# Bias relus with the first weight as a second scalar, in an attention and experts kernel

## The chip, the cores and the metric

The kernel runs on one core of a Trainium2 chip. The metric is device time in microseconds (us) of one execution; several executions were timed and one was profiled. PE is TensorE's matmuls, PEld its weight loads, DVE VectorE, ACT ScalarE, POOL GpSimd, and SP the engine whose queue issues the DMAs (SPq).

## The reference

Three blocks run one after the other, all in float32.

```python
scores = scale * np.matmul(q, k.transpose(0, 1, 3, 2))      # batch 2, 8 heads, 576 positions, head size 64
psi_rel = np.log1p(np.abs(rel))                             # rel = i - j
psi_i = np.log1p(np.maximum(pos[:, None], 1.0))
x = (psi_rel / psi_i)[..., None]
h = np.maximum(x @ w1 + b1, 0.0)                            # 32 hidden values
bias = h @ w2                                               # one bias per head, row i and column j
attn = softmax(scores + bias);  out = attn @ v
# then, on 1152 tokens of 512 values:
x = sum over 4 experts of p[e] * (relu(x @ w1[e]) @ w2[e])  # 1024 hidden values each
result = ((x @ w_a) * (x @ w_b)) @ w_out                    # 1536 hidden values
```

The change lies in the bias. Since the bias of row i depends on |i − j| alone, one row needs a table of log1p(0 ... 575). The kernel takes the division by psi_i out of the relu: max(t·w1/psi_i + b1, 0) is max(t·w1, −b1·psi_i)/psi_i + b1. So a row's relu is a maximum of the scaled table with one number per hidden value; the second matmul follows, then the factor 1/psi_i and a correction w2·b1 that is the same for all rows.

## The kernel before

**Bias units.** A unit is 16 rows i, of 36 units. Its hidden values lie on the 128 partitions as 4 rows i of 32 values each, so a unit takes four relus (`bias_group`, lines 367 to 378), each on `n` columns of the table; n falls from 576 (unit 0) to 304 in the middle and rises again to 576. In units 0 to 7 every even one has its fourth relu on ScalarE, with the other three on VectorE; the odd ones have all four on VectorE; later units have three and one. The buffers of the relus (`hh`) are eight. TensorE multiplies by `w2s` into PSUM (`pb`, line 390), an engine copies one side out with the row factor `rinv` and the correction `corr` (`put`, lines 408 and 410), another mirrors the other side (`mirror`, line 239), and a DMA on SP's queue stores the unit to memory (line 421). Attention loads tiles of it back (`bt`, lines 476 to 487) and adds them in the reduction of line 516.

**Constants.** One DMA brings `cs`: the table `tab`, the values psi_i (`neg_`), the row factors `rinv`, the two columns `cw` (w1 and b1) and `w2s`. ScalarE scales the whole table by w1 (line 345). VectorE makes the ScalarE biases `pos` (line 340), the VectorE bounds `neg_`, in place (line 341), and multiplies `w2s` by 8 (line 342), since the scores are kept eight times as large. TensorE then multiplies `w2s` by b1 (line 353), and VectorE copies that into `corr`, one vector for units with one relu on ScalarE and one for units with none, in which the quarter of ScalarE's row is set to 0 (lines 357 to 359). The relus of both engines wait for both the scaled table and the bounds.

**Order.** A planner (`Plan.run`, line 147) simulates the five engines with written costs and due times (`op`, with `prio`) and emits each engine's instructions in the order it finds; on the chip every engine works through its own list in that order and waits on semaphores. Bias units 0 to 7 have the highest rank, then 8 to 15, then the rest, which are mixed with attention steps (line 513 on) and with the experts (`up` line 772, the activation's low half `hl` line 796, weight splits `wl` line 658, `pz` line 785). From about 70 us on TensorE's list is filled with expert matmuls.

Of the kernel before, what the change touches and what calls it, by code (L numbers as in the profile page):

```python
# [9 lines left out]
F32 = mybir.dt.float32  # L10
U32 = mybir.dt.uint32
F32R = mybir.dt.float32r
AF = mybir.ActivationFunctionType
ALU = mybir.AluOpType
# [3 lines left out]
B, H, S, D = 2, 8, 576, 64  # L18
HID = 32
P = 128  # L20
# [21 lines left out]
ENGINES = {"kcast": "ACT DVE", "ksub": "POOL DVE", "qcast": "DVE", "qsub": "DVE", "pt": "ACT DVE", "tail": "ACT DVE", "side": "ACT DVE", "mirror": "POOL ACT", "mirror0": "ACT DVE",  # L42
           "whi": "ACT DVE", "wlo": "DVE", "xhi": "DVE", "xlo": "POOL DVE", "rb": "ACT DVE", "rx": "ACT DVE", "s64": "DVE",
           "wsum": "POOL DVE", "whi2": "ACT", "wlo2": "DVE", "px": "ACT DVE", "xsum": "DVE", "xhi2": "ACT", "xlo2": "DVE", "hmul": "DVE", "hlo": "DVE"}
# [49 lines left out]
class Plan:  # L94
# [9 lines left out]
    def op(self, eng, fn, r=(), w=(), rw=(), hold=(), prio=0, lock=False, after=(), size=0, late=0):  # L104

        o = Op()
        o.eng, o.fn, o.prio, o.lock, o.size = eng, fn, prio, lock, size
        o.after, o.n, o.done, o.late = [], len(self.ops), False, late
        deps = set(after)
        for b in r:  # L110
            deps.update(b.writers)
        for b in rw:
            deps.update(b.writers)
            deps.update(b.readers)
        for b in rw:
            b.writers, b.readers = [o], []
        for b in w:
            b.writers.append(o)
        for b in r:
            b.readers.append(o)  # L120
        deps.discard(o)
        o.left = len(deps)
        for d in deps:
            d.after.append(o)
        o.bufs = list({id(b): b for b in (*r, *w, *rw, *hold)}.values())
        for b in o.bufs:
            b.left += 1
        self.ops.append(o)
        return o
# [102 lines left out]
def tile_kernel(ctx, tc, qd, kd, kf, vd, cst, probs, w1r, w2r, war, wbr, wor, out):  # L232
    nc = tc.nc
    plan = Plan()
    op = plan.op
    engine = {"ACT": nc.scalar, "DVE": nc.vector, "POOL": nc.gpsimd}

    def copy(e, out, in_):
        (nc.scalar.copy if e == "ACT" else engine[e].tensor_copy)(out, in_)  # L239
# [10 lines left out]
    def t_psum(n, engs="ACT DVE"):  # L250
        est = {"ACT": n / 1.2 + 55, "DVE": n / 0.96 + 68}
        return {e: est[e] for e in engs.split()}

    def tp(stack, name, **kw):
        return stack.enter_context(tc.tile_pool(name=name, bufs=1, reuse_waits="tile", **kw))
# [29 lines left out]
    hp = tp(hp_stack, "hp", side="right")  # L285
# [45 lines left out]
    NG = S // 4  # L331
    cs_t = hp.tile([P, S + NG + NU + 2 + 32], F32, name="cs")
    cs, pos = Buf(t=cs_t), hp.tile([P, NU, max(RELUS.values())], F32, name="pos")
    corr = {n: hp.tile([P, 1], F32, name=f"corr{n}") for n in range(max(RELUS.values()) + 1)}
    tab, neg_ = cs_t[:, 0:S], cs_t[:, S:S + NG]
    rinv, cw, w2s = cs_t[:, S + NG:S + NG + NU], cs_t[:, S + NG + NU:S + NG + NU + 2], cs_t[:, S + NG + NU + 2:]
    op({"SP": 440}, lambda e: nc.sync.dma_start(out=cs_t, in_=cst), w=[cs], size=P * 3160)

    def scales(e):
        nc.vector.tensor_scalar(out=pos, in0=neg_.rearrange("p (u g) -> p u g", g=4)[:, :, 4 - pos.shape[2]:], scalar1=cw[:, 1:2], scalar2=None, op0=ALU.mult)  # L340
        nc.vector.tensor_scalar(out=neg_, in0=neg_, scalar1=cw[:, 1:2], scalar2=-1.0, op0=ALU.mult, op1=ALU.mult)
        nc.vector.tensor_scalar(out=w2s, in0=w2s, scalar1=8.0, scalar2=None, op0=ALU.mult)

    lg = Buf(t=cs_t)
    op({"ACT": S / 1.2 + 200}, lambda e: nc.scalar.activation(out=tab, in_=tab, func=AF.Copy, scale=cw[:, 0:1]), r=[cs], w=[lg], prio=-1)
    op({"DVE": 450}, scales, r=[cs], w=[lg])
    cs = lg
    pc, cr = new("tv", "pc"), Buf(t=cs_t)


    def corr_mm(e):
        for g in range(4):
            nc.tensor.matmul(pc.t[32 * g:32 * g + 32, 0:1], w2s, cw[:, 1:2], start=True, stop=True)

    def corr_copy(e):
        for n, x in corr.items():
            nc.vector.tensor_copy(x, pc.t[:, 0:1])
            for g in range(4 - n, 4):
                nc.vector.memset(x[32 * g:32 * g + 32], 0.0)

    def dist(u):
        before, after = 16 * u + 15, S - 16 * u
        return before, after, max(before + 1, after)
# [3 lines left out]
    def bias_group(u, rank):  # L367
        pri, acts = RANK[rank], RELUS[rank] if u % 2 == 0 or rank != "bias0" else 0
        before, after, n = dist(u)
        hs = []  # L370
        for g in range(4):
            G = 4 * u + g
            hh = new("hh")
            hs.append(hh)
            if g < 4 - acts:
                op({"DVE": n / 1.92 + 130}, lambda e, hh=hh, G=G: nc.vector.tensor_scalar(out=hh.t[:, :n], in0=tab[:, :n], scalar1=neg_[:, G:G + 1], scalar2=None, op0=ALU.max), r=[cs], w=[hh], prio=pri, lock=True)  # L376
            else:
                op({"ACT": n / 1.2 + 220}, lambda e, hh=hh, G=G: nc.scalar.activation(out=hh.t[:, :n], in_=tab[:, :n], func=AF.Relu, bias=pos[:, u, g - 4:][:, :1]), r=[cs], w=[hh], prio=pri)
        pb = new("tv" if n <= 512 else "s", "pb")
        bst = new("bst")  # L380


        def base():
            return (pb.t, 0) if n <= 512 else (pb.t.rearrange("p a b -> p (a b)"), 512 - n // 2)

        def mm(e):
            t, o = base()
            for lo, hi in ((0, n),) if n <= 512 else ((0, n // 2), (n // 2, n)):
                for g in range(4):
                    nc.tensor.matmul(t[32 * g:32 * g + 32, o + lo:o + hi], w2s, hs[g].t[:, lo:hi], start=True, stop=True)  # L390

        op({"PE": n * 1.67 + 170}, mm, r=[*hs, cs], w=[pb], hold=[bst], prio=pri)


        def ends():
            t, o = base()
            b = bst.t
            if before >= after:
                side = b[:, 0:before + 1], t[:, o:o + 1 + before][:, ::-1]
                rest = b[:, before + 1:before + after], b[:, before - after + 1:before][:, ::-1]  # L400
            else:
                side = b[:, before:before + after], t[:, o:o + after]
                rest = b[:, 0:before], b[:, before + 1:2 * before + 1][:, ::-1]
            return side, rest

        def put(e, out, src):
            if e == "ACT":
                nc.scalar.activation(out=out, in_=src, func=AF.Identity, scale=rinv[:, u:u + 1], bias=corr[acts])  # L408
            else:
                nc.vector.tensor_scalar(out=out, in0=src, scalar1=rinv[:, u:u + 1], scalar2=corr[acts], op0=ALU.mult, op1=ALU.add)  # L410

        def mirror(e):
            copy(e, *ends()[1])

        m = min(before, after - 1)
        side = op({e: v + 95 for e, v in t_psum(n, ENGINES["side"]).items()}, lambda e: put(e, *ends()[0]), r=[pb, cr], w=[bst], prio=pri)
        op({e: v for e, v in {"POOL": 2 * m + 150, "ACT": m / 1.2 + 95, "DVE": m / 0.96 + 68}.items() if e in ENGINES["mirror0" if rank == "bias0" else "mirror"].split()}, mirror, w=[bst], after=[side], prio=pri)
        rows.append(Buf(t=bias_d))

        def store(e):  # L420
            nc.sync.dma_start(out=bias_d[16 * u:16 * u + 16, :, S - before:S + after].rearrange("i h j -> (i h) j"), in_=bst.t[:, :before + after])

        o = op({"SP": 440}, store, r=[bst], w=[rows[u]], prio=pri, size=P * 4 * (before + after))
        if u == P // 16 - 1:
            early.append(o)
# [707 lines left out]
    for b in range(B):  # L1133
        QK[0, b, 0] = plain(0, b)
    op({"PE": 600}, corr_mm, r=[cs], w=[pc])
    op({"DVE": 400}, corr_copy, r=[pc], w=[cr])
    for u in range(NU):
        bias_group(u, "bias0" if u < P // 16 else "bias1" if u < 256 // 16 else "bias2")
    for g in groups:
# [225 lines left out]
```

## Time and profile before

| | us |
|---|---|
| median of 3 timed executions | 791.68 (790.96 to 793.36) |
| the profiled execution, its own time | 791.38 |
| its span, first to last instruction | 789.6 |
| PE busy | 774.2 (98%) |
| PEld busy | 662.3 (84%) |
| DVE busy | 649.5 (82%) |
| ACT busy | 404.3 (51%) |
| POOL busy | 28.1 (4%) |

A matmul is pipelined and the end of one is modelled, so a busy PE isn't PE at its peak. The busy share is a mean over stages: in the first 70 us bias and attention follow each other over all engines; behind 300 us PE multiplies expert and output weights almost alone. Lines such as L376 are those of the kernel before.

### The profile page before, as it was taken

The page shows a single profiled execution, that of the slowest core. Times are in us where ns is not written, and L with a number is a line of the kernel's source. Part 1 is how long each engine was busy: PE and PEld are TensorE (multiplying, and loading weights), DVE is VectorE, ACT ScalarE, POOL GpSimd, SP SyncE. Part 2 cuts the span into 40 slices and gives each one's busy share as a digit, 9 for nine tenths or more (in the row PEclk, how much of TensorE's full clock was granted, in tenths as well). Part 3 has the DMA queues.
Part 4 walks back from the last instruction along what each step waited for, and adds up shares of the span by engine and source line. Part 5 has one row for each costly group of instructions (what it writes and reads, how often), then busy time and mean ns, then how long its engine had stood idle before and what let it go on. Part 6 is the DMA issues. An engine that isn't in the chain of part 4 may idle for free.

```text
span 789.6 us, 13146 instructions
## 1 busy us (share of the span) xinstructions
PE 774.2 (98%) x4933; PEld 662.3 (84%) x4933; DVE 649.5 (82%) x1374; ACT 404.3 (51%) x848; POOL 28.1 (4%) x46
## 2 busy tenths in 40 slices
PE   7998999999999999999999999999999999999997
PEld 3475678888988888888888888889889999999996
DVE  7899986889896687998989998988698985757545
ACT  6877765677766543544544535344466532433321
POOL 0000100000000000000000000010010100000000
PEclk9999999999999999999999999999999999999999
DMA  6996658677563134455545653545405340301103
GB/s 233 327 344 215 232 178 276 218 243 244 179 208 98 45 96 127 134 166 175 160 126 159 204 175 120 166 132 161 134 1 183 112 160 1 107 27 55 54 1 120
DMA packets 46432, 120.31 MB, mean 152 GB/s; under 512 B 5024, under 2 KB 9376, under 8 KB 46368
## 3 DMA queue, kind: packets, MB, share of 16 engines
q1 hardware_dynamic: 46224, 119.34, 46.6%
q8 instruction: 39, 0.64, 0.3%
q14 instruction: 25, 0.20, 0.1%
q10 hardware_dynamic: 144, 0.13, 0.0%
HBM read 93.62 MB, written 25.84 MB: 151 GB/s over the span
## 4 chain that ended last, share of the span: by engine, by line
PE 90%; DVE 6%; ACT 1%; issue 1%; DMA 1%; DVEq 0%; ACTq 0%
PE pz L785 32%; PE up L883 14%; PE pw L1030 9%; PE up L772 8%; PE pb L390 4%; PE pv L613 4%; PE pr L1030 4%; PE ps L513 4%; PE pt L548 4%; PE pq L1030 2%; PE ps L531 1%; PE pz L1110 1%; DVE pr L516 1%; DVE k L453 1%; PE rp L593 1%
## 5 line engine op out<-in xcount | busy, mean ns | idle before, releaser
L785 PE MATMUL pz<-wh,hh 128*128 128x512 f32 x386 | 153.2, 397 | 0.0
L785 PE MATMUL pz<-wh,hl 128*128 128x512 f32 x386 | 151.3, 392 | 0.0
L785 PE MATMUL pz<-wl,hh 128*128 128x512 f32 x386 | 151.2, 392 | 0.0
L785 PEld LDWEIGHTS pz<-wl,hh 128*128 128x128 f32 x386 | 72.5, 188 | 15.9
L785 PEld LDWEIGHTS pz<-wh,hh 128*128 128x128 f32 x386 | 72.5, 188 | 14.2 <-issue 1.8
L785 PEld LDWEIGHTS pz<-wh,hl 128*128 128x128 f32 x386 | 72.5, 188 | 12.2
L239 ACT COPY ct<-pw 128x640 f32<-128x640 f32 (+3 forms) x48 | 27.9, 582 | 85.0 <-PE pw L1030 85.0
L516 DVE CUSTOM_DVE_ANT_0 pr<-ps,bt 128x576 f32<-128x576 f32 (+1 forms) x80 | 59.9, 753 | 13.9 <-PE ps L513 11.3
L658 DVE TENSOR_TENSOR wl<-wst,wh 128x1024 fp32r<-128x1024 f32 (+1 forms) x60 | 69.7, 1162 | 1.9 <-ACT wh L239 1.6
L526 ACT ACTIVATE pr<-pr,sums 128x576 f32<-128x576 f32 x72 | 56.1, 780 | 15.3 <-DVE sums L516 10.4
L772 PE MATMUL up<-x_h,wh 128*128 128x256 f32 (+1 forms) x200 | 61.7, 308 | 0.7 <-DVE hl L796 0.7
L239 ACT CAST wh<-wst 128x1024 fp32r<-128x1024 f32 (+1 forms) x56 | 54.5, 974 | 15.1 <-PE pz L785 7.8
L772 PE MATMUL up<-x_h,wl 128*128 128x256 f32 (+1 forms) x200 | 57.3, 286 | 0.0
L772 PE MATMUL up<-x_l,wh 128*128 128x256 f32 (+1 forms) x200 | 57.2, 286 | 0.0
L239 ACT COPY ptb<-pt 128x512 f32<-128x512 f32 (+3 forms) x98 | 40.3, 438 | 30.8 <-PE pt L548 25.4
L376 DVE TENSOR_SCALAR hh<-cs 128x560 f32<-128x560 f32 (+17 forms) x112 | 43.9, 448 | 3.8 <-PE pb L390 3.6
L239 ACT COPY ct<-up 128x448 f32<-128x448 f32 x39 | 20.7, 531 | 47.8 <-PE up L883 47.6
L613 PE MATMUL pv<-ptb,v 128*64 128x128 f32 (+2 forms) x480 | 44.1, 331 | 0.3 <-ACT bst L408 0.3
L883 PE MATMUL up<-xb,wsh 128*128 128x448 f32 x156 | 44.3, 365 | 0.0
L1125 DVE TENSOR_TENSOR acc<-pz,acc 128x512 f32<-128x512 f32 x44 | 30.2, 689 | 15.9 <-PE pz L785 14.9
L772 PEld LDWEIGHTS up<-x_h,wh 128*128 128x128 f32 x200 | 37.6, 188 | 6.5 <-issue 3.0
L548 PE MATMUL pt<-ident,pr 128*128 128x128 f32 x288 | 41.7, 275 | 0.0
(194 smaller groups left out, 1844.8 us busy)
## 6 DMA issues: line engine op xcount, KB each, us to landing
wst<-in_w1r SPq DMA_DIRECT2D x30, 512.0 KB, 4.4
wst<-in_w2r SPq DMA_DIRECT2D x30, 512.0 KB, 4.5
bias_d<-bst SPq DMA_DIRECT2D x36, 295.5 KB, 4.1
bt<-bias_d SPq DMA_DIRECT2D x15, 576.0 KB, 5.3
v<-in_vd SPq DMA_DIRECT2D x24, 320.0 KB, 4.3
s<-in_war SPq DMA_DIRECT2D x12, 512.0 KB, 4.9
wz_d<-hl SPq DMA_DIRECT2D x24, 256.0 KB, 2.5
s<-in_wbr SPq DMA_DIRECT2D x12, 512.0 KB, 4.9
```

The costliest lines, as they stand in the source:

```text
L239: (nc.scalar.copy if e == "ACT" else engine[e].tensor_copy)(out, in_)
L376: op({"DVE": n / 1.92 + 130}, lambda e, hh=hh, G=G: nc.vector.tensor_scalar(out=hh.t[:, :n], in0=tab[:, :n], scalar1=neg_[:, G:G + 1], sca ...
L390: nc.tensor.matmul(t[32 * g:32 * g + 32, o + lo:o + hi], w2s, hs[g].t[:, lo:hi], start=True, stop=True)
L516: nc.vector.tensor_tensor_reduce(out=pr.t[r0:r1, c].rearrange("p (a b) -> p a b", a=2), in0=ps.t[r0:r1, :, :HS], in1=bt.t[r0:r1, c].rearra ...
L526: nc.scalar.activation(out=pr.t[:, c], in_=pr.t[:, c], func=AF.Exp, scale=-1.0, bias=sums.t[:, neg:neg + 1], accum_out=sums.t[:, col:col + 1])
L548: nc.tensor.transpose(pt.t[:, kt * P:kt * P + P], pr.t[:, s, k0:k0 + P], ident)
L613: nc.tensor.matmul(pv.t[s * D:(s + 1) * D, :w], V.t[:, s, kt * D:(kt + 1) * D], ptb.t[:, blk, :w], start=(kt == 0), stop=(kt == 4))
L658: op(t_two(1024 - skip, ENGINES["wlo"]), lambda e: engine[e].tensor_tensor(out=w.t[1][:, skip:], in0=wst.t[:, skip:], in1=f(w.t[0][:, skip ...
L772: nc.tensor.matmul(u.t[:, :n], block(a, ft, d), x_at(x, d, lo, n), start=(d == 0 and j == 0), stop=(d == 3 and j == 2))
L785: nc.tensor.matmul(z.t, a[:, ft, tt * P:(tt + 1) * P], bb[:, ft, :], start=(first and ft == 0 and j == 0), stop=(final and ft == 1 and j = ...
L883: nc.tensor.matmul(bank.t[:, :n], s(a, k), x(b, k), start=(first and k == 0 and i == 0), stop=(stop and k == 1 and i == 2), skip_group_che ...
L1030: nc.tensor.matmul(o_, s[:, k], d[:, k], start=(first and k == 0 and i == 0), stop=(k == 1 and i == 2), skip_group_check=True)
```

## The change

Relus take the unscaled table and two scalars per partition: on VectorE a product with w1 and the maximum in one instruction, on ScalarE the activation's scale. The pass that scales the table goes. The bounds get a tile of their own (`neg`), made by VectorE; `pos` is made by ScalarE; the two no longer make one buffer with the table, so VectorE's relus wait for `neg` alone and ScalarE's for `pos` alone. The factor 8 moves from `w2s` to `rinv` and to the copy of the correction. GpSimd sets the correction vectors to 0 ahead of time, and the copy leaves the zero quarter out. Line numbers behind it fall by 3.

```diff
@@ -336,15 +336,11 @@
     rinv, cw, w2s = cs_t[:, S + NG:S + NG + NU], cs_t[:, S + NG + NU:S + NG + NU + 2], cs_t[:, S + NG + NU + 2:]
     op({"SP": 440}, lambda e: nc.sync.dma_start(out=cs_t, in_=cst), w=[cs], size=P * 3160)
 
-    def scales(e):
-        nc.vector.tensor_scalar(out=pos, in0=neg_.rearrange("p (u g) -> p u g", g=4)[:, :, 4 - pos.shape[2]:], scalar1=cw[:, 1:2], scalar2=None, op0=ALU.mult)
-        nc.vector.tensor_scalar(out=neg_, in0=neg_, scalar1=cw[:, 1:2], scalar2=-1.0, op0=ALU.mult, op1=ALU.mult)
-        nc.vector.tensor_scalar(out=w2s, in0=w2s, scalar1=8.0, scalar2=None, op0=ALU.mult)
-
-    lg = Buf(t=cs_t)
-    op({"ACT": S / 1.2 + 200}, lambda e: nc.scalar.activation(out=tab, in_=tab, func=AF.Copy, scale=cw[:, 0:1]), r=[cs], w=[lg], prio=-1)
-    op({"DVE": 450}, scales, r=[cs], w=[lg])
-    cs = lg
+    psi, neg_ = neg_, hp.tile([P, NG], F32, name="neg")
+    NEG, POS, RI = Buf(t=neg_), Buf(t=pos), Buf(t=cs_t)
+    op({"DVE": 220}, lambda e: nc.vector.tensor_scalar(out=neg_, in0=psi, scalar1=cw[:, 1:2], scalar2=-1.0, op0=ALU.mult, op1=ALU.mult), r=[cs], w=[NEG], prio=-1)
+    op({"ACT": 220}, lambda e: nc.scalar.activation(out=pos, in_=psi.rearrange("p (u g) -> p u g", g=4)[:, :, 4 - pos.shape[2]:], func=AF.Copy, scale=cw[:, 1:2]), r=[cs], w=[POS], prio=-1)
+    op({"DVE": 90}, lambda e: nc.vector.tensor_scalar(out=rinv, in0=rinv, scalar1=8.0, scalar2=None, op0=ALU.mult), r=[cs], w=[RI], after=[], prio=0.1)
     pc, cr = new("tv", "pc"), Buf(t=cs_t)
 
 
@@ -352,11 +348,12 @@
         for g in range(4):
             nc.tensor.matmul(pc.t[32 * g:32 * g + 32, 0:1], w2s, cw[:, 1:2], start=True, stop=True)
 
+    for n, x in corr.items():
+        nc.gpsimd.memset(x, 0.0)
+
     def corr_copy(e):
         for n, x in corr.items():
-            nc.vector.tensor_copy(x, pc.t[:, 0:1])
-            for g in range(4 - n, 4):
-                nc.vector.memset(x[32 * g:32 * g + 32], 0.0)
+            nc.vector.tensor_scalar(out=x[:P - 32 * n], in0=pc.t[:P - 32 * n, 0:1], scalar1=8.0, scalar2=None, op0=ALU.mult)
 
     def dist(u):
         before, after = 16 * u + 15, S - 16 * u
@@ -373,9 +370,9 @@
             hh = new("hh")
             hs.append(hh)
             if g < 4 - acts:
-                op({"DVE": n / 1.92 + 130}, lambda e, hh=hh, G=G: nc.vector.tensor_scalar(out=hh.t[:, :n], in0=tab[:, :n], scalar1=neg_[:, G:G + 1], scalar2=None, op0=ALU.max), r=[cs], w=[hh], prio=pri, lock=True)
+                op({"DVE": n / 1.92 + 130}, lambda e, hh=hh, G=G: nc.vector.tensor_scalar(out=hh.t[:, :n], in0=tab[:, :n], scalar1=cw[:, 0:1], scalar2=neg_[:, G:G + 1], op0=ALU.mult, op1=ALU.max), r=[cs, NEG], w=[hh], prio=pri, lock=True)
             else:
-                op({"ACT": n / 1.2 + 220}, lambda e, hh=hh, G=G: nc.scalar.activation(out=hh.t[:, :n], in_=tab[:, :n], func=AF.Relu, bias=pos[:, u, g - 4:][:, :1]), r=[cs], w=[hh], prio=pri)
+                op({"ACT": n / 1.2 + 220}, lambda e, hh=hh, G=G: nc.scalar.activation(out=hh.t[:, :n], in_=tab[:, :n], func=AF.Relu, scale=cw[:, 0:1], bias=pos[:, u, g - 4:][:, :1]), r=[cs, POS], w=[hh], prio=pri)
         pb = new("tv" if n <= 512 else "s", "pb")
         bst = new("bst")
 
@@ -413,7 +410,7 @@
             copy(e, *ends()[1])
 
         m = min(before, after - 1)
-        side = op({e: v + 95 for e, v in t_psum(n, ENGINES["side"]).items()}, lambda e: put(e, *ends()[0]), r=[pb, cr], w=[bst], prio=pri)
+        side = op({e: v + 95 for e, v in t_psum(n, ENGINES["side"]).items()}, lambda e: put(e, *ends()[0]), r=[pb, cr, RI], w=[bst], prio=pri)
         op({e: v for e, v in {"POOL": 2 * m + 150, "ACT": m / 1.2 + 95, "DVE": m / 0.96 + 68}.items() if e in ENGINES["mirror0" if rank == "bias0" else "mirror"].split()}, mirror, w=[bst], after=[side], prio=pri)
         rows.append(Buf(t=bias_d))
 
@@ -1133,7 +1130,7 @@
     for b in range(B):
         QK[0, b, 0] = plain(0, b)
     op({"PE": 600}, corr_mm, r=[cs], w=[pc])
-    op({"DVE": 400}, corr_copy, r=[pc], w=[cr])
+    op({"DVE": 200}, corr_copy, r=[pc], w=[cr])
     for u in range(NU):
         bias_group(u, "bias0" if u < P // 16 else "bias1" if u < 256 // 16 else "bias2")
     for g in groups:
```

**Order at the start.** VectorE's first instructions; before, from the constants on:

```order
L340 TENSOR_SCALAR pos<-cs 128x36
L341 TENSOR_SCALAR cs<-cs 128x144
L342 TENSOR_SCALAR cs<-cs 128x32
L376 TENSOR_SCALAR hh<-cs 128x576 x3
L376 TENSOR_SCALAR hh<-cs 128x560 x4
L357 COPY corr_101<-pc 128x1
L357 COPY corr_102<-pc 128x1
L359 MEMSET corr_102 32x1
L376 TENSOR_SCALAR hh<-cs 128x544 x3
L376 TENSOR_SCALAR hh<-cs 128x528 x4
L376 TENSOR_SCALAR hh<-cs 128x512 x3
L376 TENSOR_SCALAR hh<-cs 128x496 x4
```

and with the change:

```order
L341 TENSOR_SCALAR neg<-cs 128x144
L343 TENSOR_SCALAR cs<-cs 128x36
L373 TENSOR_SCALAR hh<-cs,neg 128x576 x3
L373 TENSOR_SCALAR hh<-cs,neg 128x560 x4
L356 TENSOR_SCALAR corr_101<-pc 128x1
L356 TENSOR_SCALAR corr_102<-pc 96x1
L373 TENSOR_SCALAR hh<-cs,neg 128x544 x3
L239 COPY bst<-bst 128x15
L373 TENSOR_SCALAR hh<-cs,neg 128x528 x4
L373 TENSOR_SCALAR hh<-cs,neg 128x512 x3
L373 TENSOR_SCALAR hh<-cs,neg 128x496 x4
```

One small instruction fewer stands ahead of the first relu, the memset is gone, and the 15-column mirror copy of unit 0 (`bst<-bst`) now stands on VectorE behind unit 2's relus.

**Order at the first long keys.** VectorE between 60 and 66 us, where the keys `k` of the first attention step with 256 queries are cast and the rest subtracted (64x1152); before:

```order
L461 TENSOR_TENSOR ql<-q_747,qh 128x512
L376 TENSOR_SCALAR hh<-cs 128x320
L239 CAST k<-k_756 128x1152
L376 TENSOR_SCALAR hh<-cs 128x320
L453 TENSOR_TENSOR k<-k_756,k 64x1152
L618 TENSOR_TENSOR xf<-pv,rb 128x128
L376 TENSOR_SCALAR hh<-cs 128x320
L239 CAST x_h<-xf 128x128
L376 TENSOR_SCALAR hh<-cs 128x336
L621 TENSOR_TENSOR x_l<-xf,x_h 128x128
```

and with the change:

```order
L239 CAST qh<-q_748 128x512
L373 TENSOR_SCALAR hh<-cs,neg 128x320
L458 TENSOR_TENSOR ql<-q_748,qh 128x512
L239 CAST k<-k_757 128x1152
L615 TENSOR_TENSOR xf<-pv,rb 128x128
L450 TENSOR_TENSOR k<-k_757,k 64x1152
L239 CAST x_h<-xf 128x128
L239 CAST k<-k_767 128x1152
L618 TENSOR_TENSOR x_l<-xf,x_h 128x128
```

Three relus that stood between the key's instructions are gone from here, and a second cast of keys, which ScalarE had, stands among them.

**Order ahead of the first expert activation.** VectorE between 66 and 71 us, with the reduction `pr,sums`, the gates (`pn`, `gate`) and the activation's low half `hl`; before:

```order
L516 ISA pr,sums<-ps,bt 128x576
L516 ISA sums 128x1
L376 TENSOR_SCALAR hh<-cs 128x336 x2
L647 TENSOR_REDUCE pn<-gate 128x9
L648 TENSOR_SCALAR pn<-pn 128x9
L649 RECIPROCAL pn<-pn 128x9
L650 TENSOR_TENSOR gate<-gate,pn 128x36
L376 TENSOR_SCALAR hh<-cs 128x352 x3
L796 SCALAR_TENSOR_TENSOR hl<-up,hh 128x256
L239 COPY ptb<-pt 128x4x128
L796 SCALAR_TENSOR_TENSOR hl<-up,hh 128x256
L658 TENSOR_TENSOR wl<-wst,wh 128x1024
```

and with the change:

```order
L513 ISA pr,sums<-ps,bt 128x576
L513 ISA sums 128x1
L373 TENSOR_SCALAR hh<-cs,neg 128x320 x2
L644 TENSOR_REDUCE pn<-gate 128x9
L645 TENSOR_SCALAR pn<-pn 128x9
L646 RECIPROCAL pn<-pn 128x9
L647 TENSOR_TENSOR gate<-gate,pn 128x36
L793 SCALAR_TENSOR_TENSOR hl<-up,hh 128x256
L655 TENSOR_TENSOR wl<-wst,wh 128x1024
L793 SCALAR_TENSOR_TENSOR hl<-up,hh 128x256
L373 TENSOR_SCALAR hh<-cs,neg 128x336 x3
```

`hl` stands ahead of three relus of the next units, which follow behind the second `hl`; the units in question are earlier ones than before (336 columns in place of 352 and 368).

## Rows read from the trace of the kernel before

**Rows 1.** Chain of waits, 0 to 30 us: start us, us, what it ran in.

```profile
4.02 0.79 ACT cs L345
...
5.41 11.94 PE pb L390 x89
```

**Rows 2.** Busy us by stretch: PE, PEld, DVE, ACT, POOL; granted clock, DMA share, GB/s.

```profile
28.00:55.00 27.00, 25.80 (x242) 17.90 (x242) 25.79 (x93) 22.29 (x57) 0.85 (x2) 1.00 1.01 369
55.00:70.00 15.00, 12.63 (x137) 9.87 (x136) 14.74 (x37) 11.95 (x27) 0.41 (x1) 1.00 0.70 237
70.00:121.00 51.00, 51.00 (x391) 35.62 (x391) 45.38 (x100) 36.66 (x69) 5.83 (x10) 1.00 0.61 207
```

**Rows 3.** Groups by shape, VectorE: line, operation, shapes, count | busy us, mean ns.

```profile
L697 DVE TENSOR_SCALAR t<-s 128x512 uint32<-128x512 uint32 x36 | 15.2, 423 | 0.5
...
L239 DVE COPY ptb<-pt 128x512 f32<-128x512 f32 x15 | 10.3, 687 | 0.2
...
L376 DVE TENSOR_SCALAR hh<-cs 128x512 f32<-128x512 f32 x6 | 2.6, 480 | 0.2 <-PE pb L390 0.2
...
L376 DVE TENSOR_SCALAR hh<-cs 128x304 f32<-128x304 f32 x6 | 2.1, 373 | 0.0
...
L937 DVE TENSOR_SCALAR acc<-pz,gate 128x512 f32<-128x512 f32 x2 | 1.5, 748 | 1.6 <-PE pz L785 1.6
...
L410 DVE TENSOR_SCALAR bst<-pb,cs,corr 128x528 f32<-128x528 f32 x1 | 0.8, 822 | 0.0
L410 DVE TENSOR_SCALAR bst<-pb,cs,corr 128x464 f32<-128x464 f32 x1 | 0.8, 761 | 0.3 <-ACT bst L408 0.3
```

**Rows 4.** The same view for ScalarE.

```profile
L239 ACT CAST hh<-ct 128x512 fp32r<-128x512 f32 x12 | 7.5, 623 | 5.5 <-DVE ct L1061 2.8 <-DVE ct L1055 2.5
...
L935 ACT ACTIVATE acc<-pz,gate 128x512 f32<-128x512 f32 x7 | 4.8, 691 | 3.5 <-PE pz L785 3.5
...
L408 ACT ACTIVATE bst<-pb,corr,cs 128x512 f32<-128x512 f32 x2 | 1.6, 778 | 6.4 <-DMA wst<-in_w2r 6.2 <-PE pb L390 0.2
...
L378 ACT ACTIVATE hh<-cs,pos 128x512 f32<-128x512 f32 x2 | 1.4, 718 | 0.0
```

**Rows 5.** Timeline, 4 to 9 us: start us, us, engine, instruction [idle before].

```profile
4.31 0.29 DVE L341 TENSOR_SCALAR cs<-cs 128x144 f32<-128x144 f32 x1
4.52 0.18 DVE L342 TENSOR_SCALAR cs<-cs 128x32 f32<-128x32 f32 x1
...
4.83 3.06 DVE L376 TENSOR_SCALAR hh<-cs 128x576 f32<-128x576 f32 x7
...
7.81 0.21 DVE L357 COPY corr<-pc 128x1 f32<-128x1 f32 x2
...
8.18 2.19 DVE L376 TENSOR_SCALAR hh<-cs 128x544 f32<-128x544 f32 x5
```

**Rows 6.** Timeline, 18 to 29 us, VectorE, ScalarE and the DMA queue SPq.

```profile
18.17 0.76 DVE L410 TENSOR_SCALAR bst<-pb,cs,corr 128x464 f32<-128x464 f32 x1 [0.27 <-ACT bst L408]
...
18.96 0.30 ACT L239 COPY bst<-bst 128x127 f32<-128x127 f32 x1
...
24.21 0.61 SPq L487 DMA_DIRECT2D bt<-bias_d  x1
...
28.15 0.76 DVE L516 CUSTOM_DVE_ANT_0 pr<-ps,bt 128x576 f32<-128x576 f32 x1 [1.96 <-DMA bt<-bias_d]
```

**Rows 7.** Busy us and count of the VectorE relus (L376) by stretch.

```profile
4.00:18.17 14.17, 12.62 (x31) 1.00 0.67 261
18.17:28.00 9.83, 6.22 (x18) 1.00 0.77 241
28.00:55.00 27.00, 4.20 (x12) 1.00 1.01 369
```

**Rows 8.** The page, part 5: the VectorE relus as one group.

```profile
L376 DVE TENSOR_SCALAR hh<-cs 128x560 f32<-128x560 f32 (+17 forms) x112 | 43.9, 448 | 3.8 <-PE pb L390 3.6
```

**Rows 9.** DMA issues, 17 to 30 us: count, KB each, median us to landing.

```profile
bias_d<-bst SPq DMA_DIRECT2D x9, 295.5 KB, 4.2
```

## The prediction

> **What bounds the kernel now.** I read the chain of waits first, then the busy time by stretch, then groups and timeline at the places that the change touches. The chain begins with the constants' DMA; at 4.02 us ScalarE scales the table for 0.79 us, and from 5.41 us the chain stands on the bias matmuls [rows 1]. The first relu of VectorE starts at 4.83 us, right behind that scaling, and nothing but its own relus fills the engine: seven in 3.06 us [rows 5]. Up to 28 us the bias units are made, 31 VectorE relus before line 410 at 18.17 us and 18 behind it [rows 7]; then the first attention reduction (line 516) waits for a bias load until 28.15 us with VectorE idle for 1.96 us [rows 6]. From 28 to 55 us VectorE is busy for 25.79 of 27 us, from 55 to 70 us for 14.74 of 15 while TensorE idles 2.37 us. From 70 to 121 us TensorE is busy all the time, at granted clock 1.00, and VectorE idles 5.6 us of 51 [rows 2]. Behind 121 us no bias work is left and TensorE carries the rest. So the change can matter in three ways: when the first relu starts, how long a relu takes, and which order the planner then makes. What is late at 70 us stays late at the end.
>
> **The price of a second scalar.** No row of before is a VectorE relu with two per-partition scalars, so the price comes from neighbours. From SBUF at 512 columns, a tensor_scalar with one immediate takes 423 ns and the relu, with one per-partition scalar, 480 ns: 57 ns for that scalar. From PSUM a plain copy of 512 columns takes 687 ns and line 937, with one such scalar, 748 ns: 61 ns. Line 410 has two: 761 ns at 464 columns and 822 ns at 528, so about 0.95 ns a column, and some 807 ns at 512: another 59 ns [rows 3]. I take **0.06 us for the second scalar**. Bounds: 0, if it is read beside the first, and the 1x rate of the PSUM rows, if two scalars cost the engine its double rate (see the rivals). A second operation costs nothing: line 341 multiplies twice with one per-partition scalar, and takes 0.29 us at 144 columns [rows 5], where the relus' own line (480 ns at 512, 373 ns at 304 columns, 0.51 ns each) [rows 3] gives 0.29. Instructions overlap by 0.08 us whatever they are (line 342 starts 0.21 us behind 341, which takes 0.29) [rows 5], so the 0.06 us appears in full in the distance from one relu to the next. On ScalarE the cast from SBUF takes 623 ns and the relu, with one per-partition operand, 718 ns; from PSUM it is 691 ns with one and 778 ns with two [rows 4]. I take 0.09 us for each of its 32 relus.
>
> The Trainium skill, page "VectorE: DVE Perf Modes", section "The TRN2 errata — SBUF-src ops pay a fixed extra latency per instruction", gives a VectorE operation one fixed cost and its columns over the rate, with no term for scalar operands. By that rule the new relus take what the old ones took; that is the second rival below. The rows above do not agree with it (423 against 480 ns).
>
> **Part by part.**
> - *Start.* The 0.79 us of ScalarE in front of the first VectorE relu goes [rows 1]. In its place VectorE computes the negated biases (the form of line 341, 0.29 us) and then scales 36 row factors (near line 342, 0.18 us), the second starting 0.21 us behind the first [rows 5]. From 4.02 us: 0.21 + 0.18, and the relu at about 4.40 us in place of 4.83: **−0.43**. Bounds −0.5 and 0 (nothing, if TensorE, which the chain names here, catches up no sooner). ScalarE's own small table of 36 elements ends about when VectorE starts, and delays only its one relu of the first unit. The correction's matmuls no longer wait for VectorE; they are 8 of one column.
> - *Correction.* Between the last relu before it and the next lie 0.37 us (7.81 to 8.18) [rows 5]; without the memset and the wait in front of it I take 0.27: −0.1, bounds −0.2 and 0. GpSimd's two memsets run before the constants land and wait for nobody; uncovered they would be some 0.2 us. The planner in turn gives the first mirror copy of 15 columns to VectorE: +0.1, bounds 0 and 0.4, since it waits there for ScalarE's copy out with the later relus behind it. The factor 8 moved from one small instruction to another: 0.
> - *Relus to line 410.* 31 × 0.06 = +1.86; with the start and the two tenths, line 410 is 1.43 us later. Its mirror ends at 19.26 us on ScalarE. The load at 24.21 us waits for that unit's store; with 4.2 us from issue to landing [rows 9] the store was issued at 20.0, 0.74 us after it could have been, because the queue SPq was still busy with an earlier load and store. So the load, and line 516 behind it, are **+0.7** later, at 28.85 us. VectorE gets there in time: it was free at 26.19 us [rows 6], plus 1.43, plus 18 × 0.06 = 1.08, is 28.70. The waiting reduction has three relus and every later attention tile queued behind it on VectorE. Bounds 0 (second scalar free) and +1.4.
> - *28 to 55 us.* 12 relus [rows 7] × 0.06 = 0.72, on an engine that idles 1.2 of 27 us. I take half, **+0.36**; bounds 0 and 0.72.
> - *55 to 70 us.* Here the planner's order changes. Three of nine relus stay; six of about 0.33 us (with the overlap off) go behind the first expert activation, but the second key cast comes from ScalarE to VectorE, and the queries' cast moves. TensorE idles here, waiting for keys and reductions on VectorE. **0**; bounds −2.37, all of TensorE's idle time, and +0.5.
> - *70 to 121 us.* 112 relus in all [rows 8], less 31, 18, 12 and 3, leave 48 × 0.06 = 2.88. VectorE's 5.6 idle us would hold it, but relus come in runs of three to six, and the expert halves and weight splits queued behind them are what TensorE waits for next. I take a quarter, **+0.72**; bounds 0 and 2.88. ScalarE's 0.09 each fall on an engine with 14 us of idle time here: 0.
>
> Sum: 0.7 + 0.36 + 0 + 0.72 = +1.8 us. The profiled execution took 791.38 us (span 789.6), 0.3 under the median of the runs, 791.68; the sum on the median gives **793.5 us**.
>
> **The rivals.**
> - *Second scalar free.* The rows of lines 937 and 410 speak against it; for it, that no SBUF row has two. Then −0.43 − 0.1 + 0.1 remain: 791.2.
> - *Nothing covers the relus (slower).* Place: the runs of relus from 28 us on. If TensorE's queue has no finished work in stock, it waits for each unit: 0.7 + 0.72 + 0.18 (three relus from 55 to 70) + 2.88 = 4.5, so 796.2. It decides from the point at which a run of relus, three to six of them, is longer than the matmuls queued ahead of its unit. For it: VectorE is busy for 98% of 55 to 70 us; against it: TensorE has no idle time from 70 to 121 us [rows 2].
> - *Double rate lost.* A relu takes 448 ns on the mean [rows 8], of which some 234 stream columns; at one column per ns it would grow by as much: 26 us of VectorE, of which the first 49 relus (12 us) are hardly covered and a third of the rest, 5 us: about 808. Line 341 kept the rate with two operations; no row has two scalars.
> - *The order gains.* If the new order fills TensorE's 2.37 us of idle time from 55 to 70 us, and the second scalar costs next to nothing: −0.43 − 2.3, so 789.0. For it: the activation is six relus earlier; against it: the key cast is a move onto the fuller engine.
>
> **How the numbers follow.** A measurement of this kernel tells 0.3%, 2.4 us, from no change. The forecast, with the scalar priced and mostly covered, has 0.50 and its own range is 792.0 to 795.0, of which 0.20 lies above 794.06. Second scalar free 0.17, nothing covers 0.19, rate lost 0.04, order gains 0.10. Slower: 0.20 + 0.19 + 0.04 = 0.43; same: 0.30 + 0.17 = 0.47; faster: 0.10. The range 790.2 to 797.2 leaves out the order's gain, the lost rate and a little at its upper end.
>
> **What would show it.** VectorE's relus of 512 columns at 540 ns, ScalarE's at 808; first relu near 4.40 us; line 410 near 19.6; the first reduction near 28.85; TensorE idle time from 70 to 121 us of under 1 us, by VectorE's relus or what stands behind them. Relus at 480 ns, or a first reduction before 28.2 us, would prove it wrong at its root; 0.7 us of TensorE idle time more or less behind 121 us would mean that the new order, not the price, decided.

## The result, and the profile after

The changed kernel takes **797.64 us** (797.42 to 797.79, 6 runs) against 792.71 (790.96 to 794.94, 6 runs) for the kernel before, run beside it: ratio 1.0065, 95% interval 1.0052 to 1.0078, so by the ratio 5.1 us slower (4.1 to 6.2). The forecast was 793.5, its range 790.2 to 797.2. The profiled execution took 797.55 us, its span is 795.8.

The price of a relu is the forecast one. The changed kernel's groups by shape, VectorE (as [rows 3]) and ScalarE (as [rows 4]):

```profile
L373 DVE TENSOR_SCALAR hh<-cs,neg 128x512 f32<-128x512 f32 x6 | 2.9, 537 | 0.2 <-PE pb L387 0.2
L373 DVE TENSOR_SCALAR hh<-cs,neg 128x304 f32<-128x304 f32 x6 | 2.4, 432 | 0.0
...
L375 ACT ACTIVATE hh<-cs,pos 128x512 f32<-128x512 f32 x2 | 1.6, 806 | 0.0
```

57 to 59 ns more on VectorE at both widths (480 and 373 before), so the rate per column is kept; 88 ns more on ScalarE (718). The page's group of all VectorE relus (as [rows 8]):

```profile
L373 DVE TENSOR_SCALAR hh<-cs,neg 128x560 f32<-128x560 f32 (+17 forms) x112 | 50.2, 502 | 1.3 <-PE pb L387 1.2
```

6.3 us more busy time, but the idle time ahead of them falls from 3.8 to 1.3 us: part of the price takes the place of waits for TensorE. The timeline of the changed kernel at the places of [rows 5] and [rows 6]:

```profile
4.35 0.18 DVE L343 TENSOR_SCALAR cs<-cs 128x36 f32<-128x36 f32 x1
...
4.47 3.49 DVE L373 TENSOR_SCALAR hh<-cs,neg 128x576 f32<-128x576 f32 x7
...
18.84 0.74 DVE L407 TENSOR_SCALAR bst<-pb,cs,corr 128x464 f32<-128x464 f32 x1
19.51 4.90 DVE L373 TENSOR_SCALAR hh<-cs,neg 128x432 f32<-128x432 f32 x12
...
21.24 3.60 POOL L239 COPY bst<-bst 128x143 f32<-128x143 f32 x2 [19.86 <-ACT bst L405]
...
24.60 0.80 SPq L418 DMA_DIRECT2D bias_d<-bst  x2
...
25.56 0.60 SPq L484 DMA_DIRECT2D bt<-bias_d  x1
...
29.79 0.76 DVE L513 CUSTOM_DVE_ANT_0 pr<-ps,bt 128x576 f32<-128x576 f32 x1 [2.44 <-DMA bt<-bias_d]
...
30.66 1.48 PE L528 MATMUL ps<-kq 64*128 64x288 f32 x8 [1.91 <-issue]
```

Line 407 is only 0.67 us later than line 410 was, yet the second bias load is 1.35 later and the first reduction 1.64. The store of line 407's own unit isn't what held the load: it went out at 19.94 us, against 19.90 before. Between them stands what neither the prediction nor the rows ahead of it name: **GpSimd's mirror copy of 143 columns** (unit 8), which starts at 21.24 us inside VectorE's unbroken run of twelve relus. GpSimd's groups by shape from 17 to 31 us, the changed kernel:

```profile
L239 POOL COPY bst<-bst 128x143 f32<-128x143 f32 x1 | 3.3, 3333 | 19.9 <-ACT bst L405 19.9
...
L239 POOL COPY bst<-bst 128x175 f32<-128x175 f32 x1 | 0.3, 328 | 0.0
```

and the kernel before:

```profile
L239 POOL COPY bst<-bst 128x143 f32<-128x143 f32 x1 | 0.4, 407 | 19.5 <-ACT bst L408 19.5
...
L239 POOL COPY bst<-bst 128x175 f32<-128x175 f32 x1 | 0.3, 335 | 2.2 <-ACT bst L408 2.2
```

The same copy took 0.41 us before and takes 3.33 now, from 21.24 to 24.57, just past the end of the run at 24.41; the larger copy behind it, in a pause of VectorE, takes 0.33. The store of that unit goes out at 24.60 (before, the timeline has it at 21.22), and the load of 25.56 stands behind it on SP's queue. TensorE idles 1.91 us, and then this happens in the changed kernel (busy us and granted clock by stretch, columns as in [rows 2]):

```profile
28.00:32.00 4.00, 2.09 (x11) 0.77 (x10) 2.21 (x7) 1.87 (x4) 0.37 (x1) 1.00 1.00 356
32.00:33.00 1.00, 1.00 (x8) 0.93 (x7) 1.00 (x4) 0.78 (x3) 0.00 (x0) 0.74 1.03 395
33.00:34.00 1.00, 1.00 (x6) 0.67 (x6) 0.97 (x6) 0.96 (x3) 0.00 (x0) 0.50 1.05 329
34.00:35.00 1.00, 1.00 (x6) 0.72 (x6) 0.70 (x3) 1.00 (x3) 0.00 (x0) 0.50 0.96 356
35.00:36.00 1.00, 1.00 (x5) 0.24 (x4) 0.81 (x3) 0.15 (x2) 0.00 (x0) 0.55 1.05 413
...
55.00:70.00 15.00, 12.80 (x141) 9.61 (x138) 14.82 (x36) 9.91 (x21) 0.00 (x0) 1.00 0.83 281
70.00:121.00 51.00, 50.35 (x379) 33.77 (x379) 48.73 (x107) 41.64 (x83) 2.08 (x4) 1.00 0.64 208
121.00:300.00 179.00, 177.46 (x1349) 153.67 (x1349) 144.15 (x321) 111.99 (x266) 6.62 (x11) 1.00 0.52 170
```

The granted clock, 1.00 there before [rows 2], is 0.50 (1.2 in place of 2.4 GHz) from 32.5 to 36 us. Behind that, TensorE idles 2.20 us from 55 to 70 (2.37 before), 0.65 from 70 to 121 (none before) and 1.54 from 121 to 300, where the kernel before idles 0.87; from 300 us to the end it idles 5.21, against 5.51.

So the theory to test, **held copy**: the run of relus keeps GpSimd's copy out, the load and the first reduction come late, TensorE idles and loses its clock. Its rivals: the relus' price alone, and the planner's new order.

### The profile page after: what moved, and what is told of

Read it like the earlier page. It is cut to its first block, busy times and chain, and to the rows that moved or that the text cites. A ratio compares the mean times of both kernels' runs of the same rounds, so it can differ in the third digit from the quotient of the medians.

```text
span 795.8 us, 13142 instructions
## 1 busy us (share of the span) xinstructions
PE 779.2 (98%) x4933; PEld 662.2 (83%) x4933; DVE 652.8 (82%) x1373; ACT 407.9 (51%) x853; POOL 31.4 (4%) x42
## 4 chain that ended last, share of the span: by engine, by line
PE 91%; DVE 4%; ACT 2%; DMA 1%; issue 1%; DVEq 0%; ACTq 0%
PE pz L782 33%; PE up L880 14%; PE pw L1027 9%; PE up L769 8%; PE pv L610 5%; PE pr L1027 5%; PE ps L510 4%; PE pb L387 4%; PE pt L545 4%; PE pq L1027 2%; PE ps L528 1%; DVE hh L373 1%; DVE wl L655 1%; PE pz L1107 1%; DMA wst<-in_w1r 1%
## 5 line engine op out<-in xcount | busy, mean ns | idle before, releaser
L239 ACT CAST wh<-wst 128x1024 fp32r<-128x1024 f32 (+1 forms) x59 | 57.0, 967 | 13.5 <-PE pz L782 7.7
L239 ACT COPY ptb<-pt 128x512 f32<-128x512 f32 (+3 forms) x94 | 38.6, 437 | 28.5 <-PE pt L545 21.9
L373 DVE TENSOR_SCALAR hh<-cs,neg 128x560 f32<-128x560 f32 (+17 forms) x112 | 50.2, 502 | 1.3 <-PE pb L387 1.2
L792 ACT ACTIVATE hh<-up 128x256 fp32r<-128x256 f32 (+2 forms) x76 | 27.8, 381 | 32.5 <-PE up L769 24.7
```

## The experiments

Only g2 and g3 move other instructions than those that the edit names. `ones` is a column of ones that GpSimd writes at the start. Medians stand with the ratio to the kernel before, run beside them (median 791.48 in the runs of e, 791.92 of f, 791.53 of g). Beside the changed kernel it was 792.71, so what an experiment gains on the changed kernel is 0.8 to 1.2 us less by the ratios than by the medians; where it matters, both are given.

**e1: the changed kernel's order with one scalar per relu.**

```diff
-... scalar1=cw[:, 0:1], scalar2=neg_[:, G:G + 1], op0=ALU.mult, op1=ALU.max)
+... scalar1=1.0, scalar2=neg_[:, G:G + 1], op0=ALU.mult, op1=ALU.max)
-... func=AF.Relu, scale=cw[:, 0:1], bias=...
+... func=AF.Relu, bias=...
```

> The changed kernel, in its order, with the first weight left out of the relus (an immediate 1.0 on VectorE, no scale on ScalarE): the bias is computed without that weight. Relus go back to 480 ns (VectorE) and 718 ns (ScalarE) at 512 columns. Theory 'held copy' (the unbroken run of twelve relus of two scalars keeps GpSimd's 143-element copy out for 3.3 us, the second bias load and the first reduction are late by 1.6 us, TensorE idles and its clock falls): with shorter relus the copy takes about 0.4 us again, the first reduction comes near 28.0, no clock of 0.50 behind 32 us. Time 792 if the rest of the loss is the price of the relus too. Rival 'order' (the planner's new order behind 55 us is worth the other half of the loss, whatever a relu costs): the first 55 us recover, the end does not: 795.5 to 796.

792.49 us, ratio 1.0014 (1.0006 to 1.0023). About four fifths of the loss go with the second scalar (0.14% are left of 0.65%); VectorE's relus of 512 columns are back at 482 ns. But in the profiled run, the second longest of twelve (793.88), the copy is held at one scalar as well. GpSimd's group by shape in e1:

```profile
L239 POOL COPY bst<-bst 128x143 f32<-128x143 f32 x1 | 2.5, 2460 | 18.1 <-ACT bst L405 18.1
```

and the timeline, VectorE, GpSimd and TensorE:

```profile
18.69 3.12 DVE L373 TENSOR_SCALAR hh<-cs,neg 128x416 f32<-128x416 f32 x9
...
19.51 2.93 POOL L239 COPY bst<-bst 128x143 f32<-128x143 f32 x2 [18.13 <-ACT bst L405]
...
29.36 1.48 PE L528 MATMUL ps<-kq 64*128 64x288 f32 x8 [2.87 <-issue]
```

So a run of relus of one scalar can hold the copy too, for 2.46 us, which I had not expected. It is held as long as the run lasts: it ends at 21.97 us, 0.16 behind the last relu (21.81), as in the changed kernel (24.57 and 24.41). The first reduction comes at 28.49 us. Of the other eleven runs there is no trace, so whether their copy was held isn't shown. TensorE idled 2.87 us in the profiled run, with the clock at 1.00 all the way behind it, so an idle stretch alone doesn't make the clock fall.

**e2: the order of before with a second scalar in every relu.**

```diff
-... scalar1=neg_[:, G:G + 1], scalar2=None, op0=ALU.max)
+... scalar1=ones, scalar2=neg_[:, G:G + 1], op0=ALU.mult, op1=ALU.max)
-... func=AF.Relu, bias=...
+... func=AF.Relu, scale=ones, bias=...
```

> The kernel before, in its order, with a second per-partition scalar (a column of ones) as a multiplier in every relu, VectorE and ScalarE. Relus at 540 and 811 ns. Theory 'held copy': here too GpSimd's 143-element copy is kept out of VectorE's run of twelve, 3 us in place of 0.41, the first reduction 1.5 to 2 us later, a clock of 0.50 behind it: +5, about 797.5, with no change of order at all. Rival 'order': only what was lost up to 55 us, +3: about 795.8. Rival 'price only' (each relu 0.06 us longer, nothing else): first reduction +1.0, no fall of the clock, +2 to +3: about 795.

796.03 us, ratio 1.0059 (1.0045 to 1.0074): by the ratios the second scalar makes 4.7 of the 5.1 us with no change of order; by the medians e2 lies 1.6 us under the changed kernel. VectorE's relus of 512 columns take 546 ns. GpSimd's group by shape in e2:

```profile
L239 POOL COPY bst<-bst 128x143 f32<-128x143 f32 x1 | 3.3, 3327 | 20.3 <-ACT bst L408 20.3
```

The first reduction comes at 30.11 us (28.15 before), with no fall of the clock in the profiled run. Of the six runs three have a mean granted clock of 0.999 (795.2 to 795.6) and three of 0.997 or 0.998 (796.4 to 797.5). The median is nearer to the number of the rival "order" (795.8) than to 797.5, but that rival has no held copy: the copy was held and the reduction late, and what is missing is the fall of the clock, which at least three of the six runs do not have.

**e3: the changed kernel, that one copy on ScalarE.**

```diff
-            copy(e, *ends()[1])
+            copy("ACT" if u == 8 else e, *ends()[1])
```

> The changed kernel with that one 143-element copy issued on ScalarE in the place that the planner gave it; everything else in the same order. Theory 'held copy': the store goes out 2 us earlier, the second bias load at about 24.6 in place of 25.56, the first reduction near 28.9 (from 29.79), TensorE idles about 1 us less, the clock stays at 1.00: 797.6 less 0.9 and less 1.5 for the clock, about 795. Rival 'price only': nothing hangs on the copy, 797.6 within 0.5.

793.79 us, ratio 1.0031 (1.002 to 1.0042): one instruction moved takes back 3.85 us by the medians (797.64 less 793.79) and 2.7 by the ratios, where 2.6 was expected. The timeline, SP's queue and VectorE:

```profile
23.19 0.61 SPq L484 DMA_DIRECT2D bt<-bias_d  x1
...
27.45 0.76 DVE L513 CUSTOM_DVE_ANT_0 pr<-ps,bt 128x576 f32<-128x576 f32 x1 [0.40 <-DMA bt<-bias_d]
```

The first reduction is 2.34 us earlier than in the changed kernel, even 0.70 earlier than before, and waits only 0.40 us for the load.

**e4: work for TensorE where it idles.**

```diff
+..., [nc.tensor.matmul(pb.t[...], w2s, tab[:, 0:512], start=True, stop=True) for g in range(4 * 2) if u == 13]
```

> The changed kernel with two repeated bias-like units of matmuls (8 of 512 columns, into a tile that has been read already) put on TensorE where it idles before the first reduction. GpSimd's copy is as long as before (3.3 us) and the first reduction as late (29.8), but TensorE has work from 28.75 to about 30.7. Theory 'the clock falls because of the idle stretch': granted clock 1.00 from 32 to 36 us, the time 797.6 less about 1, 796.5. Rival 'the clock falls for another reason, or its fall is covered': clock 0.50 again, or the time the same within 0.5.

795.62 us, ratio 1.0056 (1.0042 to 1.007). TensorE's timeline in e4:

```profile
28.31 1.95 PE L405 MATMUL pb<-cs 128*32 128x512 f32 x16
30.21 1.48 PE L528 MATMUL ps<-kq 64*128 64x288 f32 x8
```

No idle time is left ahead of the attention matmuls of 30.21 us, the clock is 1.00, and the copy still takes 3330 ns. Five of six runs lie at 795.49 to 795.66; the sixth, with a mean clock of 0.997, takes 797.16. So the fall of the clock costs about 1.5 us here, and as much in e2 (its two groups of three). Against the changed kernel, all six of whose runs have 0.997 or 0.998, e4 gains 2.0 us by the medians and 0.7 by the ratios, whose intervals overlap. The held copy is worth what is left to e3, run in the same set: 1.8 us.

**f1 to f4: copy on ScalarE in all, to price the rest.** f1 is the kernel before with e3's line; f2 is e1 with it, f3 is e2 with it; f4 is f3 with the second scalar in the later units alone:

```diff
-... scalar1=ones, scalar2=neg_[:, G:G + 1], op0=ALU.mult, op1=ALU.max)
+... **(dict(scalar1=ones, scalar2=neg_[:, G:G + 1], op0=ALU.mult, op1=ALU.max) if u > 14
+       else dict(scalar1=neg_[:, G:G + 1], scalar2=None, op0=ALU.max)))
-... func=AF.Relu, scale=ones, bias=...
+... func=AF.Relu, **(dict(scale=ones) if u > 14 else {}), bias=...
```

> The kernel before with its 143-element mirror copy on ScalarE in place of GpSimd. If the copy is a matter of luck in the kernel before too (it slipped between two relus in the profiled run; e1's profiled run, of relus as short, held it for 2.46 us), taking it from GpSimd removes the slower runs: median 791.0, runs within 1 us of each other. If it always slips in there, ScalarE's 0.3 us are all that changes: 791.5 within 0.3.

> The changed kernel's order with one scalar per relu (the first weight left out of the bias) and the 143-element copy on ScalarE: beside f1 it gives what the new order and the earlier start are worth without held copy and without the second scalar. If the order costs nothing: as f1, 791 or 0.4 below. If the order behind 55 us costs: up to 1 more, 792.

> The order of before with a second scalar (ones) in every relu and the 143-element copy on ScalarE: beside f1 it gives the price of the second scalar alone. The prediction's own terms for it (0.7 to the first reduction plus the 0.43 us of start that this kernel does not have, 0.36 and 0.72 behind it) make +2.0 to +2.2: 793.2. If nothing covered it, 0.06 for each of 112 relus: +5 or more, 796. No clock of 0.50 behind 30 us.

> As f3, but the second scalar only in the relus of the units made behind the first reduction (unit 15 on); the first 15 units have one scalar. The prediction's terms: 0.36 + 0.72 = +1.1 against f1, 792.1. If the relus behind 28 us are all covered, as f1; if none of them is, 60 relus at 0.06, +3.5.

| | us | ratio to before (95%) |
|---|---|---|
| f1: one scalar, order of before | 790.88 | 0.9988 (0.9979 to 0.9997) |
| f2: one scalar, order of the change | 792.60 | 1.0009 (1.0001 to 1.0017) |
| f3: two scalars, order of before | 793.80 | 1.0027 (1.0017 to 1.0037) |
| e3: two scalars, order of the change | 793.79 | 1.0031 (1.002 to 1.0042) |
| f4: f3, second scalar from unit 15 on | 792.80 | 1.0012 (1.0004 to 1.0021) |

With the copy out of the way the second scalar costs 2.9 us in the order of before (f3 less f1): 1.0 in the first 15 units and 1.9 behind them (f4 less f1). I had expected 2.0 to 2.2 and 1.1. The new order with its earlier start costs 1.7 (f2 less f1), where I had allowed 1; the two don't add (e3 less f1 is 2.9, or 3.4 by the ratios, not 4.6). f1 beats both kernels, by 1.0 us over the one before; its runs spread over 1.6 us, more than I expected, so the copy was not the only reason for the spread. The clock is another: in f1's profiled run (792.07 us) it falls to 0.50 from 64.2 to 67.6 us, behind a stretch of 60 to 64 us in which TensorE idles 1.70 us, and in f2's (793.28) from 63.3 to 66.7. f1's stretch, as in [rows 2]:

```profile
55.00:70.00 15.00, 12.93 (x123) 9.80 (x118) 13.59 (x36) 10.61 (x23) 0.41 (x1) 0.89 0.64 223
```

The kernel before has this too: 22 of its 75 runs beside the experiments have a mean clock of 0.998, and take 1.3 us more on the mean than the other 53 (792.70 and 791.36).

The waits of TensorE from 100 to 300 us show a part of what the order loses; f2:

```profile
PE up L769 <- DVE hl L793: 0.9, 3, 0.4
PE ps L510 <- DVE sums L513: 0.5, 1, 0.5
PE rp L590 <- ACT ptb L239: 0.4, 1, 0.4
```

and the kernel before:

```profile
PE up L772 <- DVE hl L796: 0.5, 1, 0.5
PE ps L513 <- DVE sums L516: 0.3, 1, 0.3
```

(us in total, times, longest.) 1.8 in place of 0.8 us: three waits for an expert activation's low half in place of one, and one for a copy out of PSUM. Within 0.1 us these waits are the same in the profiled runs of the changed kernel, e1, e3, e4 and g1, and those of the kernel before the same in e2, f1, f3, f4 and g4: they belong to the order. They make 1.0 of the 1.7 us.

**g1: pauses in the run of relus.**

```diff
-..., op0=ALU.mult, op1=ALU.max), r=[cs, NEG]
+..., op0=ALU.mult, op1=ALU.max) and u in (10, 11) and nc.vector.memset(gapt, 0.0), r=[cs, NEG]
```

> The changed kernel with a one-element memset on VectorE behind each of six relus (units 10 and 11) inside the run of twelve that holds GpSimd's copy; nothing else changes. If it is the unbroken run of relus from SBUF that keeps the copy out, the copy ends within 1 us of its start in place of 3.33, the first reduction comes near 28 us, the clock stays at 1.00, and the six memsets cost 0.2 to 0.4 us: about 794, as e3. If the copy waits for something else: 797.6 or more.

794.24 us, ratio 1.0035 (1.0024 to 1.0045), as expected. GpSimd's group by shape in g1:

```profile
L239 POOL COPY bst<-bst 128x143 f32<-128x143 f32 x1 | 0.6, 572 | 19.6 <-ACT bst L405 19.6
```

and VectorE's timeline:

```profile
20.95 0.06 DVE L373 MEMSET gap<- 128x1 f32 x1
21.34 0.49 DVE L373 TENSOR_SCALAR hh<-cs,neg 128x416 f32<-128x416 f32 x1
21.36 0.06 DVE L373 MEMSET gap<- 128x1 f32 x1
...
27.29 0.76 DVE L513 CUSTOM_DVE_ANT_0 pr<-ps,bt 128x576 f32<-128x576 f32 x1 [0.16 <-DMA bt<-bias_d]
```

Six memsets of one element, more work for VectorE, gain 3.4 us on the changed kernel by the medians, 2.4 by the ratios: the copy, from 21.00 us on, takes 0.57 us in place of 3.33, and ends 0.16 us behind the second memset (21.42). What it had waited for was a break in the run.

**g2 and g3: the planner told of the conflict.** In the kernel before (g2) and in the changed one (g3):

```diff
-... mirror, w=[bst], after=[side], prio=pri)
+... mirror, w=[bst], after=[side], prio=pri, lock=True)
```

> The kernel before with the mirror copies marked for the planner as work that must not run beside VectorE's copies and relus (lock), so that the planner itself gives the early ones to ScalarE; the order changes in many places. Theory 'held copy': at best as f1, 790.9. Rival: the planner's order elsewhere is worse by more than the luck of one copy, over 791.9.

> The same mark in the changed kernel. The 143-element copy goes to ScalarE by the plan: no held copy and no clock of 0.50 behind 32 us, so 3.85 of the 5 us come back: 793.8, as e3, plus or minus what the planner's other order is worth (1 us).

796.17 us, ratio 1.0054 (1.0039 to 1.0069), and 795.34, ratio 1.0047 (1.0032 to 1.0063). The early copy is gone from GpSimd in both, and the first reduction comes at 27.16 and 27.07 us; but the mark moves many other copies and their order, and g2 lies 5.3 us above f1, which moved one. g2 fell to its rival; g3 gains on the changed kernel, 1.5 short of what I expected. Where the new orders lose was not followed up.

**g4: the second scalar on VectorE alone**, f3 with one edit:

```diff
-... func=AF.Relu, scale=ones, bias=...
+... func=AF.Relu, bias=...
```

> As f3 (order of before, copy on ScalarE), but the second scalar in VectorE's relus alone; ScalarE's have one as before. The prediction put ScalarE's 0.09 us each at nothing: as f3, 793.8 within 0.4. If ScalarE's relus are on the path at the start: 0.5 to 1 less.

793.68 us, ratio 1.0025 (1.0015 to 1.0036), against 793.80 for f3: ScalarE's share costs nothing that can be measured.

## Why the prediction was wrong

- **Price of the second scalar: right.** 0.06 us was forecast and 0.057 to 0.059 measured on VectorE, 806 ns on ScalarE at 512 columns (808 forecast). The double rate was kept; "second scalar free" and "double rate lost" are out (the first of them is the rival that the prediction's sentence on the errata means, though it calls it the second). ScalarE's relus at nothing: right (g4).
- **Start: right.** First relu at 4.47 us (4.40), with constants landing 0.12 us later than before.
- **Relus to line 410: too high.** +0.67 where I had +1.43: the 31 relus did grow, from 12.62 us [rows 7] to 14.32, and the start was 0.36 earlier, but I let all of the growth delay it. Between the first relu and line 410 VectorE had 0.72 us in which it ran no relu; 0.05 of them were left.
- **The step that failed: "So the load, and line 516 behind it, are +0.7 later".** I followed the store of line 410's unit alone and took the load's other predecessors on SP's queue as they stood. Between that store and the load stand two more, and the first of them waits for GpSimd's copy of unit 8, of which I had no row. The store that I did follow went out only 0.04 us later (19.94). Measured: load +1.35, reduction +1.64, and behind it a fall of the clock that no case of mine had. Together 3.85 us by the medians of e3 and the changed kernel, 2.7 by the ratios: about 1.8 of it is the copy (e3 and e4), the rest, 0.9 to 2.0, the clock, whose fall costs about 1.5 among the runs of e2 and of e4.
- **What I did price, without the copy:** e3 is 2.3 us above the kernel before run beside it (793.79 less 791.48); the sum was +1.8. That the two lie so close is luck, since the parts are not as I had them. In e3 the first reduction comes 0.70 us earlier than before, not 0.7 later; against f1 the early relus cost 1.0 (forecast 0.7 with 0.43 of start already taken off), the later ones 1.9 (forecast 0.36 and 0.72).
- **55 to 70 us at nothing, and under 1 us of idle time from 70 to 121:** right (2.20 and 0.65 us). TensorE idles 0.67 us more from 121 to 300, but 0.37 more over all that lies behind 121, so the 0.7 that I named as the sign of the order did not show. The order costs something all the same, by f2 1.7 us. I had costed the order at 0 with 0.5 as its bound.
- **"Nothing covers the relus", 796.2:** nearest in its number, but for another reason. With the copy away the price is 2.9 us, not 4.5; the rest was not TensorE waiting for relus that run long, but one instruction of 143 columns that could not run beside them, and the fall of the clock.

The Trainium skill, page "SBUF — State Buffer", section "Who interferes with whom", says that VectorE in a two-port mode (which its copies, casts and tensor_scalars can enter) and GpSimd exclude each other for the whole of an instruction, whichever comes first. The traces agree, 3.33 against 0.41 us; they add that a waiting copy can lose at one boundary after another: eight relus overlap it in the changed kernel, the copy gains no entry between any two of them, and with one-element memsets between them it was done in 0.57 us (g1).

## What to carry to other kernels

Ahead of lengthening an instruction, list what else runs beside its longest unbroken run, GpSimd's small copies first, and follow each to the DMA queue behind it: the bill came from a copy of 143 columns that nothing in the engines' busy time shows. If a transfer depends on such a copy, put the copy on an engine that the run doesn't hold up (ScalarE in f1 and e3), or break the run with something tiny (g1). And look where small prices could open an idle stretch on TensorE: a first reduction 2.34 us later than in e3 came with a loss of 2.7 to 3.85 us, part of it because the clock fell behind it.

## What was not expected of the hardware

- The copy waits for a VectorE instruction to end. In all six traces in which GpSimd has it, it ends 0.16 us behind one: behind the run's last relu in the changed kernel, e1, e2 and e4, behind a memset in g1, and in the kernel before behind a relu within the run (21.03 and 21.19 us), at the first end that came. So at one scalar one trace let it in (407 ns) and one held it to the run's end (2460 ns), and at two scalars the three unbroken runs all held it (3333, 3327 and 3330 ns). Whether two scalars always shut it out, and what decides, was not settled.
- An idle stretch of TensorE does not settle whether its clock falls. 1.91 us of it (changed kernel) were followed by 0.50 from 32.5 to 35.9 us, and the mean clocks of all six runs (0.997 and 0.998) fit that, though they don't tell the place; 2.87 us (e1) and 1.79 us (e2) were not, in the profiled runs. With the stretch filled (e4) five of six runs kept the clock.
- A one-element memset between two relus costs 0.01 to 0.02 us there: the distance from relu to relu is 0.42 us at 416 columns in g1, 0.41 in the changed kernel.
